# Order of the kept chunks' dK and dV, larger stores and a regrouped last chain in a fused attention-and-MLP backward pass

## The chip, the cores and the metric

The kernel runs on one core of one Trainium2 chip. The metric is the device time of one execution in microseconds (us); times quoted are medians. Every execution of the two kernels and of the experiments fell in the fast state, with two exceptions, both of run e10, that are named there and left out of the comparison.

## The reference

The forward pass is two layers of attention and MLP, used twice with the same weights; the kernel returns the output and all gradients.

```python
# B=2, one new token each, D=1024, F=3584, 32 query heads, 4 key/value heads, 16384 cached keys, head size 128
def attn(x, K, V, wq, wo):                 # K, V: (2, 4, 16384, 128) bf16
    q = heads(x @ wq)
    p = softmax(q @ repeat(K).T * 128 ** -0.5)
    return merge(p @ repeat(V)) @ wo
def mlp(x, w1, b1, w2, b2):
    return gelu(layernorm(x) @ w1 + b1) @ w2 + b2
def f(x, K, V, wq, wo, w1, b1, w2, b2):
    for _ in range(2):
        x = x + attn(layernorm(x), K, V, wq, wo)
        x = x + mlp(layernorm(x), w1, b1, w2, b2)   # normalized here and again inside
    return x
out, vjp = jax.vjp(f, ...)
return out, *vjp(grad_out)   # output 1 = dx, 2 = dK, 3 = dV, 4 = dWq, 5 = dWo, 6..9 = dw1, db1, dw2, db2
```

dK and dV have the size of the caches (33.5 MB each). They and the weight gradients are written in the last pass over the caches, while K and V are read once more.

## The kernel before

The last pass begins at about 740 us. It works in **steps**. A step has two slots, and a streamed chunk of V (1 MB in bf16) takes four slots. There are 32 chunks. Four of them (numbers 0 to 3, the **kept** ones) are still on the chip from the pass before; the other 28 are **streamed**. For each slot PE transposes eight blocks of V, an engine copies them to `kT`, and eight products make dP. Each step also makes halves of dK chunks in its first slot and of dV chunks in its second, none, one or two in a slot as `k_at` and `v_at` below ask for it:

```python
X = [px([128, 512], F32, "xm%d" % i) for i in range(4)]      # four PSUM banks; mx() hands them out in turn

def kv_pair(w, i, h):                     # half h of chunk i of dV or dK
    g, c = chunks[i]
    if h == 0:
        stgs[w, i] = new_home()           # a 1 MB staging buffer
    ...
    pss = [mx() for _ in range(4)]        # all four banks
    for b in range(2):
        for r in range(4):
            PE.matmul(pss[r][:, b * 256:(b + 1) * 256], lhsT=blk[32 * r:32 * r + 32, o + 2 * h + b, :], ...)
    for r in range(4):
        evac_cast(sv_[:, 2 * h:2 * h + 2, r], pss[r][:]..., 512)    # a copy of 128x512, on DVE or ACT
    store(dst, <this half>, stgs[w, i] if h == 1 else None)         # 512 KB
```

The weight gradients are cut into **fill units**: one product of 128x512 into one of the same four banks, and one copy. Loads are issued by SP into whichever 1 MB buffer comes free, out of some sixteen that serve for loads and for staging alike; stores are issued by POOL. The loop, with what chooses the order:

```python
    v_at = {2 * i - 3: i for i in range(2, NC)}                  # step -> chunk of dV
    k_at = {(i - 1 if i < NCH else 2 * i - NCH - (i == NC - 1)): i for i in range(NC)}     # NCH = 4, NC = 32
    make_blks(None, 0)
    while ...:                            # m counts the steps
        for k in range(2):
            ...                           # transposes of V, kT, dP of the slot
            at, w, m_ = ((k_at, "K", m - 1), (v_at, "V", m))[k]
            for h in range(2):
                if at.get(m_ - h) is not None:
                    kv_pair(w, at[m_ - h], h)
            if tail:
                tail.popleft()()
        ...
        step_fill(1 if m < NCH else 5)    # fill units of this step
        pump(...)                         # loads, while buffers are free
        m += 1
```

The end of the pass is a chain: the last dP, the last quads of dq, their evacuation and reduction, the products `dn_tail` with Wq, a layer-norm backward, and output 1. It was driven by `sch.later(...)`, one or two steps later for each link, and by the list `tail`.

Of the kernel before, what the change touches and what calls it, by code (L numbers as in the profile page):

```python
# [9 lines left out]
BF16 = mybir.dt.bfloat16  # L10
# [13 lines left out]
def kernel(  # L24
# [25 lines left out]
    V = nc.vector  # L50
    S = nc.scalar
    PE = nc.tensor

    B, _, D = A_x.shape
# [972 lines left out]
            V.tensor_copy(out=diag[:, t], in_=gcols.unsqueeze(1).to_broadcast([128, 4, n]))  # L1027

    def q_make(w, g, bank):
        Qm = wrk2.tile([128, 2, 128], BF16, name="Qm" + w)  # L1030
        for t in range(2):
            PE.matmul(bank[:, t * 128:(t + 1) * 128], lhsT=spr[w][:, t * 128:(t + 1) * 128], rhs=ident[:],
                      start=True, stop=True)
        evac_cast(Qm[:].rearrange("p a b -> p (a b)"), bank[:, 0:256], 256)
        qms[w, g] = Qm
# [101 lines left out]
    def store(out_ap, view, tile_):  # L1137
        nc.gpsimd.dma_start(out_ap, view)
        if tile_ is not None:
            by_store.append(tile_)  # L1140
# [21 lines left out]
    def dw_units(xrows, yrows, i, chunks, y0, ny, out_of):  # L1162

        ps_, tpos = (slice(0, 128), None) if i is None else (slice(32 * i, 32 * i + 4), (32 * i, 0))
        box = {}
        units = []
        for j0, rb in chunks:
            for j in range(rb):
                for c0 in range(0, ny, 512):
                    def u(j0=j0, rb=rb, j=j, c0=c0):  # L1170
                        if j == 0 and c0 == 0:
                            box["t"] = new_home()
                        sv_ = box["t"][:, 0:rb * ny].rearrange("p (j n) -> p j n", j=rb)
                        ps = mx()
                        PE.matmul(ps[:], lhsT=xrows[ps_, (j0 + j) * 128:(j0 + j + 1) * 128],  # L1175
                                  rhs=yrows[ps_, y0 + c0:y0 + c0 + 512], start=True, stop=True, tile_position=tpos)
                        evac_cast(sv_[:, j, c0:c0 + 512], ps[:], 512)
                        if c0 + 512 >= ny and (j % 2 == 1 or j == rb - 1):
                            js = j - j % 2
                            store(out_of(j0 + js, j + 1 - js), sv_[:, js:j + 1], box["t"] if j == rb - 1 else None)  # L1180
                    units.append(Unit(u, j == 0 and c0 == 0))
        return units

# [63 lines left out]
    def kv_pair(w, i, h):  # L1247

        g, c = chunks[i]
        if h == 0:  # L1250
            stgs[w, i] = new_home()
        sv_ = stgs[w, i][:].rearrange("p (b r t d) -> p b r t d", r=4, t=2, d=128)
        blk, Qm = blks[w, i], qms[w, g]
        o = 0 if w == "V" else NB
        pss = [mx() for _ in range(4)]
        for b in range(2):
            for r in range(4):
                PE.matmul(pss[r][:, b * 256:(b + 1) * 256], lhsT=blk[32 * r:32 * r + 32, o + 2 * h + b, :],  # L1258
                          rhs=Qm[32 * r:32 * r + 32, :, :].rearrange("p a b -> p (a b)"), start=True, stop=True,
                          tile_position=(32 * r, 0))  # L1260
        for r in range(4):
            evac_cast(sv_[:, 2 * h:2 * h + 2, r], pss[r][:].rearrange("p (b t d) -> p b t d", b=2, t=2), 512)
        dst = (dVv if w == "V" else dKv)[g, :, c * TC + h * TC // 2:c * TC + (h + 1) * TC // 2, :]
        store(dst, stgs[w, i][:, h * LDW // 2:(h + 1) * LDW // 2].rearrange("p (t d) -> p t d", d=128),
              stgs[w, i] if h == 1 else None)

    dwq_v = out_4.rearrange("(j p) n -> p j n", p=128)
    quarters = {}
# [7 lines left out]
    def in_rows(q, kv):  # L1276
        box, ps = q[4], pm_([128, 512], F32, "dn_tail")

        def part(a):
            for j in range(a, a + 4):  # L1280
                for o in range(8):
                    PE.matmul(wide_out(ps, 2 * j), lhsT=box[j - j % 4][:, j % 4, o * 128:(o + 1) * 128],  # L1282
                              rhs=wide_in(dq_all[:, kv * 8 + o, 0:2]), start=(o == 0), stop=(o == 7))

        def last():
            V.tensor_tensor(out=dn0[:], in0=dn0[:], in1=pairs(ps, DJ), op=ALU.add)
            g0 = attn_in_bwd(0, g1, dn0, lambda: step_fill(1), lambda: step_fill(2))
            tail.append(lambda: col_to_row_f32(g0, DJ, out_1.rearrange("b s d -> (b s) d"), "o1",
                                               ktp.tile([128, 8, 128], BF16, name="o1", tag="kT")))

        return [lambda: part(0), lambda: part(4), last]

    def quarter(kv):

# [45 lines left out]
    def dq_quad(i, q):  # L1340
        g, c = chunks[i]
        accs[g].coef = lambda u: dX[i][:, u - c * CP, 0].rearrange("p h t -> p (h t)")
        accs[g].quad(c, q)
        if q == 1:
            if g == G - 1:
                by_read.append(held_tiles["K%d" % c])
            else:
                done("K", g, c)

    def score0(s):  # L1350
        i, b = NCH + s // NB, s % NB
        g, c = chunks[i]
        if b == 0:
            dps["t"] = pm_([128, 16, TC], F32, "dp")
        scores(i, b, kTs.pop(s), dps["t"])
        if b < NB - 1:
            return
        if c == 0:
            open_dq(g)
        if order.index(g) % 2 == 1 and c == (2 if i < 2 * NCH else 0):  # L1360
            quarter_loads(g % HKV)
        ds0(i, dps["t"][:])
        end = 1 if i == NC - 1 else 2
        sch.later(1, lambda: dq_quad(i, 0))
        sch.later(end, lambda: dq_quad(i, 1))
        if c == NCH - 1:
            sch.later(end, accs[g].evac)
            sch.later(end + 1, accs[g].reduce)

    def step_fill(n):  # L1370
        for k in range(n):
            for q in ((late, fill) if k % 2 == 0 else (fill, late)):
                if q and q[0].ready():
                    q.popleft()()
                    break
# [53 lines left out]



    v_at = {2 * i - 3: i for i in range(2, NC)}
    k_at = {(i - 1 if i < NCH else 2 * i - NCH - (i == NC - 1)): i for i in range(NC)}
    make_blks(None, 0)
    NS = (NC - NCH) * NB
    zero = {}
    m = 0
    while 2 * m < NS + 12 or late or fill or late_pe or tail or m <= max(v_at) + 2:
        sch.s = m
        qs = []  # L1440
        iv, ik = v_at.get(m + 1), k_at.get(m)
        for w, i in (("V", iv), ("K", ik)):
            if i is not None and chunks[i][1] == 0 and (w, chunks[i][0]) not in qms:
                qs.append(make_qm(w, chunks[i][0]))
        for k in range(2):
            s = 2 * m + k
            if s < NS:
                i, b = NCH + s // NB, s % NB
                cv = get("V", *chunks[i])[:].rearrange("p (t d) -> p t d", d=128)
                kT = ktp.tile([128, 8, 128], BF16, name="kT", tag="kT")  # L1450
                tp = mtp()
                for j in range(8):
                    PE.transpose(tp[:, j, :], cv[:, b * 8 + j, :], ident[:])
                evac_bf16(kT[:].rearrange("p a b -> p (a b)"), tp[:].rearrange("p a b -> p (a b)"), 1024)
                kTs[s] = kT
                if b == NB - 1:
                    done("V", *chunks[i])
                if b == 0 and chunks[i][1] == 0:
                    wg = chunks[i][0]
                    V.tensor_copy(out=wide_do[wg][:, :, 3], in_=cols["V"][:, wg].rearrange("p l r -> p (l r)"))  # L1460
            if 0 <= s - 2 < NS:
                score0(s - 2)
            if late_pe and (k == 1 or s >= NS or len(late_pe) > 6):
                late_pe.popleft()()
            at, w, m_ = ((k_at, "K", m - 1), (v_at, "V", m))[k]
            for h in range(2):
                if at.get(m_ - h) is not None:
# [3 lines that stand above are left out]
        for f in qs:  # L1471
            f()
        if iv is not None or ik is not None:
            make_blks(iv, ik)
        sch.run_slot(1)
        if m == NS // 2 - 8:
            zero["t"] = new_home()
            nc.gpsimd.memset(zero["t"][:, 0:2 * D], 0.0)
            nc.gpsimd.tensor_copy(out=zero["t"][96:100, 0:D], in_=rowsB[96:100, :])
        step_fill(1 if m < NCH else 5)  # L1480
        pump(NLD + 3 if m < NCH else NLD, 3)
        m += 1

# [29 lines left out]
```

## Time and profile before

| | before |
|---|---|
| median of 3 runs | 1141.74 us (1140.79 to 1143.36) |
| span of the profiled run, mean granted clock of PE | 1144.5 us, 0.852 |
| moved in it | 449.33 MB |
| busiest engine | PE, 83% of the span |

Three more views of this profile matter later. The first is one stretch, steps 9 to 32 of the last pass. Its columns are those of the stretches in the prediction: window, length, busy us (and instructions) of PE, PEld, DVE, ACT, POOL, then granted clock, DMA share, GB/s.

```profile
801.60:955.20 153.60, 136.13 (x1835) 84.26 (x1834) 121.48 (x216) 113.75 (x218) 41.35 (x72) 0.84 1.02 418
```

A step takes 6.4 us here (153.6 / 24), and DVE is busy for 79% of it, ACT for 74%.

The second is the list of what engines waited for from 800 us on (total us, times, longest). The two largest lines in which a copying engine waits for a store to land are these (two more, for `keepK`, have 2.3 and 2.1 us):

```profile
ACT big L161 <- DMA out_dram<-big: 15.7, 3, 11.7
DVE big L164 <- DMA out_dram<-big: 13.6, 2, 11.1
```

So before, the copies were at times ahead of the DMA and stood waiting for a free staging buffer. But none of these waits lies in steps 9 to 32: all are between 955 and 1107 us, and 11.7 and 11.1 us of them are one stall of both engines at 1061 to 1072. The third view is the summary of the chain that ended last, as shares of the span. The whole chain is short: followed back from the end it reaches only to 1105.8 us, and at 1108.3 the landing of a store holds it for 2.88 us:

```profile
PE 1%; DVE 1%; issue 0%; DMA 0%; ACT 0%; POOLq 0%; DVEq 0%; ACTq 0%
```

### The profile page before, as it was taken

The page shows a single profiled execution, that of the slowest core. Times are in us where ns is not written, and L with a number is a line of the kernel's source. Part 1 is how long each engine was busy: PE and PEld are TensorE (multiplying, and loading weights), DVE is VectorE, ACT ScalarE, POOL GpSimd, SP SyncE. Part 2 cuts the span into 40 slices and gives each one's busy share as a digit, 9 for nine tenths or more (in the row PEclk, how much of TensorE's full clock was granted, in tenths as well). Part 3 has the DMA queues.
Part 4 walks back from the last instruction along what each step waited for, and adds up shares of the span by engine and source line. Part 5 has one row for each costly group of instructions (what it writes and reads, how often), then busy time and mean ns, then how long its engine had stood idle before and what let it go on. Part 6 is the DMA issues. An engine that isn't in the chain of part 4 may idle for free. (4 is left out here: it accounts for less than half of the span.)

```text
span 1144.5 us, 40256 instructions
## 1 busy us (share of the span) xinstructions
PE 949.9 (83%) x17565; PEld 733.8 (64%) x17567; DVE 633.3 (55%) x1357; ACT 564.7 (49%) x1415; POOL 117.9 (10%) x206
## 2 busy tenths in 40 slices
PE   4988796488879875899997789889898989998586
PEld 3867674487767765888776688765555555555352
DVE  1545442133545433454845355768778877887485
ACT  0544352022535430344454454657767867777473
POOL 0000000000000000000000000012232322222323
PEclk9988886597999975899997799978878888988795
DMA  9999999998999989999999899987999999999997
GB/s 374 423 424 425 424 424 412 406 377 359 425 424 423 424 320 423 390 373 408 368 417 421 340 359 355 352 347 276 411 421 420 420 417 415 388 407 403 417 401 292
DMA packets 98717, 449.33 MB, mean 393 GB/s; under 512 B 8418, under 2 KB 8418, under 8 KB 67564
## 3 DMA queue, kind: packets, MB, share of 16 engines
q1 hardware_dynamic: 72204, 348.17, 75.6%
q0 software_dynamic: 26336, 98.60, 21.2%
q8 instruction: 137, 2.24, 0.7%
q14 instruction: 40, 0.33, 0.1%
HBM read 348.14 MB, written 98.58 MB: 390 GB/s over the span
## 5 line engine op out<-in xcount | busy, mean ns | idle before, releaser
L153 ACT COPY kT<-tp 128x512 int32<-128x512 int32 x209 | 122.7, 588 | 252.5 <-PE tp L420 246.0
L156 DVE COPY kT<-tp 128x1024 bf16<-128x1024 bf16 x159 | 108.7, 690 | 109.6 <-PE tp L420 100.4
L420 PE MATMUL tp<-ident,kv_K 128*128 128x128 bf16 x1728 | 141.3, 229 | 5.0 <-DMA kv_K<-in_A_k_cache_dram 4.6
L420 PEld LDWEIGHTS <-kv_K 128*128 128x128 bf16 x1728 | 107.1, 102 | 6.0 <-DMA kv_K<-in_A_k_cache_dram 5.3
L164 DVE CAST big<-xm 128x512 bf16<-128x512 f32 (+1 forms) x125 | 80.8, 684 | 33.2 <-DMA out_dram<-big 13.6
L161 ACT CAST big<-xm 128x512 bf16<-128x512 f32 (+1 forms) x139 | 75.6, 594 | 37.1 <-DMA out_dram<-big 15.7
L573 PEld LDWEIGHTS <-kT 128*128 128x128 bf16 x2048 | 76.0, 98 | 27.4 <-issue 21.5
L573 PE MATMUL sc<-qT_bf,kT 128*128 128x8 bf16 x2048 | 91.7, 171 | 0.3 <-issue 0.3
L270 PE MATMUL wtp<-ident,wt 128*128 128x128 bf16 x928 | 76.2, 230 | 3.7 <-issue 2.4
L420 PE MATMUL tp<-ident,kv_V 128*128 128x128 bf16 x864 | 71.1, 230 | 8.3 <-DMA kv_V<-in_A_v_cache_dram 6.8
L537 ACT ACTIVATE e_all<-sc,negm 128x64 bf16<-128x64 f32 x256 | 77.1, 345 | 1.1 <-DVE negm L532 1.0
L161 ACT CAST keepV<-xm 128x512 bf16<-128x512 f32 x118 | 64.7, 594 | 24.8 <-PE xm L1258 18.5
L306 PEld LDWEIGHTS <-wt 128*128 128x128 bf16 x1696 | 48.8, 103 | 42.6 <-issue 15.2
L452 PE MATMUL acc_all<-kv_V,e_all 128*16 128x256 bf16 x864 | 46.4, 295 | 28.5 <-DMA kv_V<-in_A_v_cache_dram 15.2
L156 DVE COPY wT<-wtp 128x1024 bf16<-128x1024 bf16 (+1 forms) x64 | 40.7, 640 | 47.7 <-PE wtp L270 44.1
L164 DVE CAST keepK<-xm 128x512 bf16<-128x512 f32 (+1 forms) x87 | 56.4, 684 | 18.3 <-PE xm L1258 9.7
L153 ACT COPY wT<-wtp 128x512 int32<-128x512 int32 (+1 forms) x60 | 34.3, 572 | 63.6 <-PE wtp L270 55.2
L164 DVE CAST keepV<-xm 128x512 bf16<-128x512 f32 x86 | 55.7, 683 | 15.1 <-PE xm L1258 8.5
L420 PEld LDWEIGHTS <-kv_V 128*128 128x128 bf16 x864 | 56.3, 103 | 10.1 <-DMA kv_V<-in_A_v_cache_dram 8.1
L270 PEld LDWEIGHTS <-wt 128*128 128x128 bf16 x928 | 58.3, 103 | 4.3 <-issue 2.9
L161 ACT CAST keepK<-xm 128x512 bf16<-128x512 f32 (+1 forms) x95 | 51.7, 590 | 18.3 <-PE xm L1258 14.2
L537 ACT ACTIVATION_READ_ACCUMULATOR e_all<-sc,negm 128x1 f32 x256 | 60.1, 235 | 0.0
(368 smaller groups left out, 1845.8 us busy)
## 6 DMA issues: line engine op xcount, KB each, us to landing
kv_K<-in_A_k_cache_dram SPq DMA_DIRECT2D x81, 1024.0 KB, 11.7
kv_V<-in_A_v_cache_dram SPq DMA_DIRECT2D x81, 1024.0 KB, 12.2
wt<-in_A_wo_dram SPq DMA_DIRECT2D x32, 1024.0 KB, 10.1
out_dram<-big POOLq DMA_DIRECT2D x62, 512.0 KB, 15.0
wt<-in_B_w_dram SPq DMA_DIRECT2D x32, 896.0 KB, 14.2
out_dram<-keepV POOLq DMA_DIRECT2D x44, 512.0 KB, 13.8
out_dram<-keepK POOLq DMA_DIRECT2D x42, 512.0 KB, 15.2
wt<-in_A_wq_dram SPq DMA_DIRECT2D x16, 1024.0 KB, 9.0
```

The lines of the kernel that those rows point to most:

```text
L153: S.copy(out=dst.bitcast(I32), in_=src.bitcast(I32))
L156: V.tensor_copy(out=dst, in_=src)
L161: S.copy(out=dst, in_=src)
L164: V.tensor_copy(out=dst, in_=src)
L270: PE.transpose(tp[:, o, :], wv[:, j, (o0 + o) * 128:(o0 + o + 1) * 128], ident[:])
L306: PE.matmul(fps[:, jo, :].rearrange("p (a b) -> p a b", b=2), lhsT=wv[:, j, jo * 128:(jo + 1) * 128], rhs=xT_bf[:, j0 + j, :].unsqueeze(1) ...
L420: PE.transpose(tp[:, j, :], cv[:, b * 8 + j, :], ident[:])
L452: PE.matmul(self.acc[cg:cg + 16, :], lhsT=coef(u), rhs=self.cv[:, t:t + 2, :].rearrange("p t d -> p (t d)"), start=False, stop=True, tile_ ...
L537: S.activation(out=e_all[:, g, f * half:(f + 1) * half, l, h, :], in_=sc[g][f][:, h, :].rearrange("p (a b) -> p a b", b=2), func=ACT.Exp, ...
L573: PE.matmul(sc[g][f][:, :, t % TH], lhsT=kT[:, j, :], rhs=q_bf[:, g, :], start=True, stop=True)
```

## The change

There are three parts. **(1)** The dV and dK of streamed chunks come first, so that the first steps turn loaded buffers over quickly; the six kept pieces that remain (dK 0 to 3, dV 2 and 3) are spread over steps 10 to 29, and the weight gradients wait until step 9. **(2)** Many stores are of 1 MB, not 512 KB. **(3)** The last chain is put into the list `tail`, which is emptied at one more place in each half step, and four unused products of 256 columns follow each piece that is taken there, to keep PE's clock up.

```diff
 def q_make(w, g, bank):
-    Qm = wrk2.tile([128, 2, 128], BF16, name="Qm" + w)
+    Qm = (vec if g == g0_ else wrk2).tile([128, 2, 128], BF16, name=("Q0" if g == g0_ else "Qm") + w)
 # dw_units
-    if c0 + 512 >= ny and (j % 2 == 1 or j == rb - 1):
-        js = j - j % 2
-        store(out_of(j0 + js, j + 1 - js), sv_[:, js:j + 1], box["t"] if j == rb - 1 else None)
+    if j == rb - 1 and c0 + 512 >= ny:
+        store(out_of(j0, rb), sv_, box["t"])
 # kv_pair
-    store(dst, <one half>, stgs[w, i] if h == 1 else None)
+    n = TC if 2 <= i < NC - 2 else TC // 2
+    if h == 1 or n < TC:
+        ...
+        store(dst, <the whole chunk, or the half>, stgs[w, i] if h == 1 else None)
 # in_rows
-    return [lambda: part(0), lambda: part(4), last]
+    return [lambda: (part(0), part(4)), lambda: None, last]
 # score0
-    end = 1 if i == NC - 1 else 2
+    if i == NC - 1:
+        tail.append(lambda: (dq_quad(i, 0), dq_quad(i, 1), accs[g].evac()))
+        tail.append(accs[g].reduce)
+        return
     sch.later(1, lambda: dq_quad(i, 0))
-    sch.later(end, lambda: dq_quad(i, 1))
+    sch.later(2 if i < NC - 2 else 1, lambda: dq_quad(i, 1))
     ...
 # the loop
-v_at = {2 * i - 3: i for i in range(2, NC)}
-k_at = {(i - 1 if i < NCH else 2 * i - NCH - (i == NC - 1)): i for i in range(NC)}
-make_blks(None, 0)
+v_at = {2 * i - 7: i for i in range(NCH, NC)}
+k_at = {2 * i - NCH - 2: i for i in range(NCH, NC)}
+for i in range(NCH):
+    k_at[9 + 6 * i] = i
+for i in range(2, NCH):
+    v_at[4 + 8 * i] = i
     ...
+            if tail:
+                tail.popleft()()
+                for _ in range(4):
+                    PE.matmul(ACCT[:, 0:256], lhsT=ident[:], rhs=<256 columns of e_all>, ...)   # result unused
             at, w, m_ = ((k_at, "K", m - 1), (v_at, "V", m))[k]
     ...
-        step_fill(1 if m < NCH else 5)
+        if NCH <= m < 2 * NCH + 1:
+            fill.popleft()()
+        step_fill(0 if m < 2 * NCH + 1 else 5)
```

More of the change, by code (lines that the diff above doesn't have):

```diff
@@ L1262, in kv_pair @@
             evac_cast(sv_[:, 2 * h:2 * h + 2, r], pss[r][:].rearrange("p (b t d) -> p b t d", b=2, t=2), 512)
-        dst = (dVv if w == "V" else dKv)[g, :, c * TC + h * TC // 2:c * TC + (h + 1) * TC // 2, :]
-        store(dst, stgs[w, i][:, h * LDW // 2:(h + 1) * LDW // 2].rearrange("p (t d) -> p t d", d=128),
-              stgs[w, i] if h == 1 else None)
+        n = TC if 2 <= i < NC - 2 else TC // 2
+        if h == 1 or n < TC:
+            t0 = h * n if n < TC else 0
+            dst = (dVv if w == "V" else dKv)[g, :, c * TC + t0:c * TC + t0 + n, :]
+            store(dst, stgs[w, i][:].rearrange("p (t d) -> p t d", d=128)[:, t0:t0 + n], stgs[w, i] if h == 1 else None)
     dwq_v = out_4.rearrange("(j p) n -> p j n", p=128)
@@ L1362, in score0 @@
         ds0(i, dps["t"][:])
-        end = 1 if i == NC - 1 else 2
+        if i == NC - 1:
+            tail.append(lambda: (dq_quad(i, 0), dq_quad(i, 1), accs[g].evac()))
+            tail.append(accs[g].reduce)
+            return
         sch.later(1, lambda: dq_quad(i, 0))
-        sch.later(end, lambda: dq_quad(i, 1))
+        sch.later(2 if i < NC - 2 else 1, lambda: dq_quad(i, 1))
         if c == NCH - 1:
-            sch.later(end, accs[g].evac)
-            sch.later(end + 1, accs[g].reduce)
+            sch.later(2, accs[g].evac)
+            sch.later(3, accs[g].reduce)
     def step_fill(n):
@@ L1464 @@
                 late_pe.popleft()()
+            if tail:
+                tail.popleft()()
+                for _ in range(4):
+                    PE.matmul(ACCT[:, 0:256], lhsT=ident[:], rhs=e_all[:, 0, 0:8, :, :, :].rearrange("p a l h t -> p (a l h t)"),
+                              start=False, stop=True, skip_group_check=True)
             at, w, m_ = ((k_at, "K", m - 1), (v_at, "V", m))[k]
```

## The prediction

> **What bounds the kernel now.** I first read the table of busy time in 40 slices: from the first slice to the last the row of the DMA stands at 9 in nearly every slice, while no engine is full throughout. So the kernel is a stream of 449 MB, and what can be won is the time in which that stream is not full. Then I cut the last pass (the one the change touches, from about 740 us) into stretches. The columns are busy time of PE, PEld, DVE, ACT and POOL, then the granted clock, the DMA share and the GB/s:
>
> ```profile
> 740.00:750.00 10.00, 8.26 (x115) 6.55 (x104) 5.87 (x16) 4.58 (x11) 1.59 (x3) 0.71 1.00 403
> 750.00:800.00 50.00, 44.85 (x637) 29.76 (x634) 38.05 (x66) 36.01 (x71) 11.59 (x21) 0.85 0.80 296
> 800.00:1107.00 307.00, 265.81 (x3572) 163.84 (x3565) 234.63 (x415) 219.58 (x421) 84.44 (x140) 0.84 1.02 411
> 1107.00:1130.00 23.00, 18.43 (x196) 8.66 (x194) 14.96 (x28) 13.40 (x26) 9.08 (x17) 0.63 0.99 400
> 1130.00:1144.50 14.50, 5.62 (x25) 1.90 (x24) 6.58 (x19) 3.69 (x7) 3.31 (x5) 0.61 0.48 195
> ```
>
> The reader is to see two holes around a full middle. Over 307 us the DMA share is 1.02 and 411 GB/s move; PE is busy 87% of it, DVE 76%, ACT 72%, so they have slack. From 750 to 800 only 296 GB/s move: 50 x (1 - 296/411) = 14.0 us of DMA time lost. From 1130 to the end 195 GB/s: 14.5 x (1 - 195/411) = 7.6 us lost. Everything else in the pass loses under 1 us. A perfect last pass would thus save about 21.6 us at the present rate.
>
> The waits of the DMA queue's own sequencer (SP) from 740 to 830 say why the first hole is there:
>
> ```profile
> SPq L1207 <- DMA out_dram<-big: 27.0, 2, 18.8
> SPq L1207 <- DMA out_dram<-keepV: 19.6, 3, 11.1
> SPq L1207 <- DMA out_dram<-keepK: 19.0, 1, 19.0
> SPq L1207 <- DMA out_dram<-keepxV: 10.2, 1, 10.2
> ```
>
> Loads (L1207) wait, up to 19 us at a time, for a store to land, because the 1 MB buffer they go into is still a staging buffer. The timeline of SP shows ten loads issued by 740.3 and then only four until 801.4 (759.8, 779.1, 789.9, 801.4). The first steps of the pass compute dK and dV of the chunks held on chip, then dW too, all of which take buffers for staging and free none by reading a streamed chunk. The same steps are long: the pairs of transposed V slots start at 749.5, 757.2, 763.8, 770.9, 777.0, 782.9, that is 6.7 us a step, with up to three half chunks of dV or dK copied in a step.
>
> The end, from the chain that ended last (start, duration, what):
>
> ```profile
> 1107.20 0.23 PE dp L1321
> ...
> 1108.26 2.88 DMA out_dram<-keepK
> ...
> 1118.53 0.99 PE xm L467 x4
> ...
> 1125.22 0.96 PE dn_tail L1282 x32
> ...
> 1127.07 0.96 PE dn_tail L1282 x32
> ...
> 1135.17 1.01 PE o L199 x4
> ```
>
> From the last dP product to the last store it is 37.3 us: 1107.2 to 1144.5. The dq reduction (L467), the two halves of the dn products and the transposes of output 1 stand with other work between them, and the clock there is 0.61 to 0.63.
>
> **What the skill says.** (1) "DMA: Bandwidth & Descriptors", section "Where 436 GB/s comes from": the ports carry 435 GB/s, and HBM may bind at some 358. Here 411 is held for 307 us, so the lower figure does not bind in this case and 411 is already 94% of the port figure: larger stores can add little. (2) The same page, "Why small descriptors are slow": a fixed overhead of about 3 cycles a packet. The packet records of this trace agree in kind: between 800 and 1130 a stored packet of 4096 B took 160.5 ns in the mean and one of 7168 B 273.5, which is 0.0368 ns a byte and 9.8 ns fixed; loads of 2048 and 8192 B (84.4, 328.0 ns) give 3.2 ns fixed. (3) "TensorE: Matmul & The Clock Gate", section "Part 1: The HAM clock gate": idle PE falls to half clock and some 3.4 us of activity bring it back. The trace agrees with the direction (0.61 in the tail, 1.00 in 690 to 740); its wake-up time I have not measured.
>
> **The change, part by part.**
>
> *Streamed chunks first.* Before, a step (two slots) up to number 4 made a dV half and up to two dK halves, all of kept chunks, and fill units began at once: one a step, five from step 4. Now steps 0 to 8 carry one dV and one dK half of streamed chunks, no dW, and only the five units that transpose rows; kept dK come at steps 9, 15, 21, 27, kept dV at 20 and 28. Copies a step in those nine steps: 8 of 128x512 at 0.684 (DVE) or 0.594 (ACT), two of 128x1024 at 0.690 or as halves 2 x 0.588, one block of the same size and a dS product of about 0.7 every other step: (8 x 0.64 + 3 x 0.75 + 0.35)/2 = 3.9 us on each engine, so with PE's waits I reckon 4.7 to 5.3 us a step in place of 6.7. Traffic a step is then 1 MB loaded and 1 MB stored: 2.1 MB / 5 us = 420 GB/s, so the DMA is about full from the moment stores flow. What stays of the hole is its start: dV0 and dV1 are stored from the same places as now, the ten early loads are done by about 750, and the first 1 MB of a streamed chunk is stored only at the end of step 2, near 757. I book 5 us lost there and 2 for steps that compute holds: 7 of the 14.0 remain, gain 7. The instruction order confirms that the same ten loads come first and that the next two go into buffers of dV0 and dV1, where before the next went into that of dK0.
>
> *Stores of 1 MB in place of 512 KB.* POOL has 64 queue rows fewer. POOL is no bound (84.4 of 307 us busy in the middle). Packets: 98.6 MB less 7.3 MB in 7 KB rows is 22,280 packets of 4 KB; some 2,050 stay, the others become 10,100 pairs, each saving 9.8 ns if the fixed part is paid once: 10,100 x 9.8 / 16 engines = 6.2 us. As 411 is so near the port figure I count half, 3 us. Against it: a buffer is held longer, by the half MB more that must land (about 2 us), and buffer V0 stays taken until step 28, one of some 16.
>
> *The tail.* The last dq quads, evacuation and reduction move from the ends of steps m+1 and m+2 into the next half steps, both dn halves are one piece (64 products), and four unused 256-column matmuls follow each piece. By the new order, from the last dP to output 1 stand 16 quads, 8 pair matmuls, the reduction, 8 + 4 transposes, 4 units, 64 products, 8 pair matmuls and 3 units. With the durations of the old chain (dq 0.8, evacuation and reduction 1.5, dq copies 0.5, rows 1.7, units 1.0, products 1.9, pairs 2, LN chain 4, transposes and copies 1.6, and waits) that is some 16 us against 30 (1107.2 to 1137.2). Behind it come 13 copies (13 x 0.64 / 2 = 4.2 us) and a last store of 1 MB, which needs about 6 us where 512 KB took 5.3 (1139.2 to 1144.5). So 26 us from last dP to end in place of 37. That is not all gain: the last dP itself comes later, since the bytes are the same and fewer stores are left behind it (I reckon 8 MB, four of them in flight, in place of 12). The measure is lost DMA time: 26 us hold 10.7 MB at 411, 8 move, 6.5 us lost, where 37.3 us lost about 8.5. Gain 2, and 1 more for the clock. The 24 unused matmuls cost 24 x 0.11 to 0.21 = 2.6 to 5 us of PE time, mostly while it waits for copies.
>
> *Sum:* 7 + 3 + 3 = 13 us off 1141.7: about **1128.5**.
>
> **Rivals.** *Buffers become the wait.* Larger stores hold buffers longer, and 11 us of PE already stand at 1061 to 1072 behind two copies that waited 11.7 and 11.1 us for stores to land. Against it: the DMA was at 1.03 during that very stall, so it cost nothing; only if it fell below full would it. It would give back some 5 to 10 us, time 1133 to 1140. *Compute becomes the bound.* The work taken out of steps 0 to 8 is added behind; PE is 87% busy. If it cannot follow, the gain of the hole is paid back later: 1136 to 1142. Against it: DVE and ACT under 77%, and PE's busy time is stretched by a clock of 0.84. Before, fill ran out near step 53 (no dW product between 1077 and the last quarter); now it should reach to the end. *The full gain.* No hole at all, the full 6 us of packets and a tail as short as its last store: 14 + 6 + 4 = 24, time 1118. For it speaks that the loads are six chunks ahead at 750. *The last store.* 1 MB behind the last copy could cost 2 us more than I booked.
>
> **Range and chances.** Most mass lies between the buffers rival and near the full gain: 1116 to 1139. Faster by over 2% means under 1119, which needs nearly all three gains whole: 0.12. Slower by over 2% needs a new stall of 36 us in a full stream: 0.02.
>
> **What would show it.** The stretch 750 to 800 at 340 to 390 GB/s, steps of about 5 us there, and more than four loads between 741 and 801; stored packets of 8192 B at about 311 ns and the middle at 414 to 418 GB/s; 24 to 28 us from last dP to end, and a clock in it above 0.65. The prediction is wrong if 750 to 800 stays at 300, if the middle shows a DMA share under 1.0 with loads waiting on stores, or if the packets of 8 KB take twice those of 4 KB.

## The result, and the profile after

| | before | changed |
|---|---|---|
| median, 4 runs each on one chip | 1142.55 us | 1157.01 us (1156.90 to 1164.02) |
| span of the profiled run, clock | 1144.5 us, 0.852 | 1155.2 us, 0.834 |

The ratio is 1.0141, with a 95% interval of 1.0098 to 1.0183. A ratio here is the mean time of one kernel's fast runs over that of the other's fast runs of the same rounds, so it is not quite the ratio of the medians. On a second chip the changed kernel gave 1.0100 (1.0064 to 1.0137; run f1 below). It is about 1 to 1.4% slower: within 2%, but 18 us above the upper end of the predicted range.

The stretches of the changed kernel that answer to the five in the prediction, cut at its own end:

```profile
740.00:750.00 10.00, 7.90 (x150) 5.67 (x147) 6.77 (x20) 5.10 (x11) 1.07 (x2) 1.00 0.93 357
750.00:800.00 50.00, 44.85 (x747) 31.66 (x743) 39.52 (x71) 37.07 (x72) 5.33 (x10) 0.90 0.90 337
800.00:1107.00 307.00, 270.61 (x3297) 162.38 (x3293) 229.87 (x396) 215.30 (x409) 49.01 (x80) 0.76 1.00 400
1107.00:1130.00 23.00, 18.83 (x276) 12.08 (x273) 16.85 (x30) 15.57 (x30) 5.26 (x9) 0.87 1.02 420
1130.00:1155.20 25.20, 12.35 (x112) 5.67 (x112) 9.89 (x23) 7.20 (x13) 3.15 (x5) 0.64 0.45 182
```

The early hole has shrunk: 337 GB/s from 750 to 800, where 296 moved before. SP's waits from 740 to 830, the view that explained the hole, are now these:

```profile
SPq L1206 <- DMA out_dram<-big: 32.6, 3, 13.3
SPq L1206 <- DMA out_dram<-keepV: 24.0, 3, 10.3
SPq L1206 <- DMA out_dram<-keepK: 20.7, 3, 9.9
```

Loads still wait for stores, no less in total, but no longer for 19 us at a time; the longest wait is 13.3, and more loads go out in between.

But the full middle is no longer full. It moves 400 GB/s in place of 411, and the clock has dropped from 0.84 to 0.76. Steps 9 to 32 of the changed kernel, the ones that now hold the kept pieces, show where:

```profile
780.80:973.60 192.80, 166.38 (x1955) 98.58 (x1956) 138.57 (x239) 129.66 (x247) 26.20 (x46) 0.71 0.98 376
```

These 24 steps begin 21 us earlier than before and end 18 us later. DVE and ACT have 52 instructions more (486 in place of 434, 12%), 48 of which must be the copies of the twelve kept halves; PE has 7% more, and the steps are 26% longer. Each engine is less busy than before: DVE 72%, ACT 67%, PE 86% (before 79%, 74%, 89%). So more work was added than fits, although no engine became full. The steps also move 72.5 MB in place of 64.2: of the 39 us by which they are longer, 20 are the time of these bytes at 411 GB/s, and the other 19 are lost. The DMA share, 0.98, hides this: a load packet of 8192 B took 366 ns in the mean in these steps, against 313 before (the median is 309 in both), so that fewer bytes kept the DMA engines nearly as busy.

The waits of the copying engines for stores, from 800 us on, in the changed kernel:

```profile
ACT big L161 <- DMA out_dram<-big: 3.0, 1, 3.0
DVE big L164 <- DMA out_dram<-big: 2.3, 1, 2.3
```

They fall from 29.3 to 5.3 us, and both lines are now in steps 9 to 32. The copies are no longer ahead of the DMA. The summary of the chain that ended last agrees. It no longer runs into the landing of a store; it goes back 243 us, to 912.4, through engines alone:

```profile
PE 14%; DVE 3%; ACT 3%; issue 1%; POOLq 0%; DVEq 0%; ACTq 0%
```

Its end, step by step (start, duration, what), answers to the chain of the prediction:

```profile
1126.32 1.04 PE xm L467 x4
...
1131.71 1.71 PE dn_tail L1283 x64
...
1139.42 1.03 PE o L199 x4
```

The last dP product is at 1121.5, so from there to the end are 33.7 us (before 37.3).

**An account of the DMA.** As in the prediction I count *lost DMA time*: the length of a stretch less the bytes moved in it at 411 GB/s. Here it is cut at the kernel's own events, and added up from the packets of one profile each. Before and the experiments e3, e6 and e11 do not differ in their opening steps, and gave 14.1, 7.6, 8.1 and 9.9 us there, so the first column is good to some 6 us only. The changed kernel and its repeat f1 agree to 0.6 us in the first three columns and differ by 3.5 in the last.

| lost, us | 740 to step 9 | steps 9 to 32 | step 33 to last dP | last dP to end | sum |
|---|---|---|---|---|---|
| before | 14.1 | -2.6 | 2.7 | 8.2 | 22.4 |
| changed | 4.8 | 16.4 | -3.2 | 13.9 | 31.9 |
| difference | -9.3 | +19.0 | -5.9 | +5.7 | +9.5 |

The difference of 9.5 us is close to that of the two profiled spans, 10.7 us; the medians of the result are 14.5 apart, since the profiled execution of before was a longer one (1146.27 us). The change won 3 to 9 us where it aimed (4.8 are left of 7.6 to 14.1), and lost more where it put the work. Behind step 33 the two last columns cancel.

### The profile page after: what moved, and what is told of

Same layout as the page of the kernel before. It is cut to its first block, busy times and chain, and to the rows that moved or that the text cites. A ratio compares the mean times of both kernels' runs of the same rounds, so it can differ in the third digit from the quotient of the medians.

```text
span 1155.2 us, 40027 instructions
## 1 busy us (share of the span) xinstructions
PE 958.4 (83%) x17577; PEld 739.7 (64%) x17579; DVE 635.2 (55%) x1355; ACT 567.2 (49%) x1418; POOL 71.7 (6%) x127
## 5 line engine op out<-in xcount | busy, mean ns | idle before, releaser
L161 ACT CAST big<-xm 128x512 bf16<-128x512 f32 (+1 forms) x150 | 80.9, 592 | 25.0 <-PE xm L1257 16.6
L164 DVE CAST big<-xm 128x512 bf16<-128x512 f32 (+1 forms) x117 | 76.2, 685 | 21.4 <-PE xm L1257 11.0
L161 ACT CAST keepV<-xm 128x512 bf16<-128x512 f32 x114 | 61.1, 591 | 27.3 <-PE xm L1257 22.9
L164 DVE CAST keepV<-xm 128x512 bf16<-128x512 f32 x93 | 60.6, 686 | 23.4 <-PE xm L1257 17.6
L161 ACT CAST keepK<-xm 128x512 bf16<-128x512 f32 x106 | 57.0, 591 | 18.6 <-PE xm L1257 15.0
L420 PEld LDWEIGHTS <-kv_V 128*128 128x128 bf16 x864 | 55.3, 102 | 13.8 <-DMA kv_V<-in_A_v_cache_dram 11.8
L164 DVE CAST keepK<-xm 128x512 bf16<-128x512 f32 x84 | 54.5, 685 | 16.4 <-PE xm L1257 11.6
## 6 DMA issues: line engine op xcount, KB each, us to landing
wt<-in_B_w_dram SPq DMA_DIRECT2D x32, 896.0 KB, 14.1
```

What stands on the lines that cost most here:

```text
L161: S.copy(out=dst, in_=src)
L164: V.tensor_copy(out=dst, in_=src)
L420: PE.transpose(tp[:, j, :], cv[:, b * 8 + j, :], ident[:])
```

## The experiments

The theory after this reading: **the kept pieces, put into steps that were already full, make compute the bound there** (the theory of compute). Its rivals are that larger stores or the longer use of buffers hold things up (buffers), that the drop of PE's clock is the cause rather than a symptom (clock), and that the unused products or the regrouped chain cost the time (tail).

### The parts alone: e1, e2, e3, e4

Four kernels ran on one chip: the larger stores alone (e1), the order alone (e2), the tail with its unused products alone (e3), order and tail without the larger stores (e4). Each takes the named hunks of the diff above and leaves the others as before.

```diff
 # e1: before, with the hunks of dw_units and kv_pair only
 # e2: before, with the hunks of q_make, v_at, k_at, make_blks and step_fill only
 # e3: before, with the hunks of in_rows, score0 and "if tail" only
 # e4: e2 and e3 together
```

> The kernel before with only the 1 MB stores. Order theory (the work moved out of the first nine steps overloads steps 9 to 32, and the stores are innocent): 1136 to 1144 us, stored 8 KB packets of about 313 ns. Buffer theory (a staging buffer held until a whole 1 MB lands starves the loads): at least 8 us slower than before, 1150 or more, with DMA share below 1.0 in the middle.

> The kernel before with only the new order of chunks and fill units (512 KB stores, old tail). Order theory: 1150 to 1160 us, steps 9 to 32 at about 8 us each as in the changed kernel. Buffer theory: the order alone fills the early hole and is faster, about 1130 us.

> The kernel before with only the new tail and the unused matmuls. Order theory: 1135 to 1143 us, last dP to end shorter than 37.3 us by some us. Tail theory (the unused matmuls sit in the way of the chain): slower by 3 us or more.

> The changed kernel with 512 KB stores back. Order theory: within 3 us of the changed kernel, 1152 to 1158 us. Buffer theory: back to 1140 or below.

| run | median us | ratio to before (95%) |
|---|---|---|
| e1 larger stores | 1144.11 | 1.0013 (0.9976 to 1.0051) |
| e2 order | 1149.95 | 1.0053 (1.0010 to 1.0097) |
| e3 tail | 1149.51 | 1.0048 (1.0005 to 1.0091) |
| e4 order and tail | 1155.02 | 1.0094 (1.0051 to 1.0137) |

The order alone is slower, and e2's profile has the changed kernel's shape: 2.6 us lost before step 9, 14.9 us in steps 9 to 32 (its six executions range from 1142.3 to 1153.8 us, and the profile is of one at 1152.2). The larger stores alone neither gain nor lose beyond the noise. The tail alone lost half a per cent in this set, but its six runs fall into two groups, near 1141 and near 1150 us (the profile is of a fast one), which I could not explain.

PE's timeline in steps 10 and 11 of e2 shows one way in which a kept piece can cost more than its work (start, duration, engine, line, operation; in brackets the idle time before it and what ended it). `Q0K` and `QmK` are the coefficients of a kept and of a streamed dK half:

```profile
785.88 0.40 PE L1258 MATMUL xm<-Q0K,blk 32*128 32x256 bf16 x8
786.94 1.48 PE L1258 MATMUL xm<-QmK,blk 32*128 32x256 bf16 x8 [0.67 <-ACT keepxK L161]
...
797.28 0.61 PE L1258 MATMUL xm<-QmK,blk 32*128 32x256 bf16 x8
798.56 1.38 PE L1258 MATMUL xm<-Q0K,blk 32*128 32x256 bf16 x8 [0.66 <-ACT keepV L161]
```

The first group of eight products takes 0.40 or 0.61 us. The second group of the same slot wants the same four banks. It stands for 0.66 us until the first copy is done, and then is paced by the copies: 1.4 to 1.5 us. During that time PE does nothing else, and the copying engines in turn wait for the products. In e2 the ten steps with a kept half (10, 11, 16, 17, 20 to 23, 28, 29) took 6.6 to 12.6 us, 99.6 together, where the same step numbers before took 5.0 to 9.5, 66.6 together: 33 of the 38 us by which steps 9 to 32 of e2 are longer. In these ten steps no engine is busier than before (PE 86% in place of 89%, DVE 67% in place of 77%, ACT 63% in place of 72%), and the granted clock is 0.50 in five of them, where it was 0.71 or more before.

### Is it the clock? e5 and e6

The granted clock in the middle of e2 is lower than before. Here PE transposes every block of V twice in steps 9 to 32, so that it is busier and a higher clock may be granted; e5 does so on e2, e6 on the kernel before.

```diff
-                for j in range(8):
+                for j in [*range(8)] * (2 if 9 <= m < 33 else 1):
                     PE.transpose(tp[:, j, :], cv[:, b * 8 + j, :], ident[:])
```

> The order alone (as e2_order) with the eight transposes of each V slot done twice, into the same place, in steps 9 to 32: 384 matmuls of 128x128 more, same result. Clock theory (in these steps PE is the bound and its granted clock of about 0.7 is the cause): the clock in 800 to 950 rises to 0.85 or more and the time falls by 4 us or more against e2_order, to 1146 or below. Overload theory (the copies and the order of work bound these steps, the clock is a by-product): the added 20 to 35 us of PE work makes it slower, 1155 or more, or leaves it as it was at a higher clock.

> The kernel before with the same doubled transposes in steps 9 to 32. Clock theory: clock up from about 0.85 to 0.95, but the DMA is full in these steps, so the time stays within 3 us of before, 1139 to 1145. Overload theory: slower by 5 us or more.

Windows 800 to 950 and 950 to 1100 of e2, then 800 to 950 of e5 (columns as above):

```profile
800.00:950.00 150.00, 131.85 (x1537) 79.66 (x1536) 105.58 (x183) 99.26 (x189) 37.07 (x65) 0.69 0.99 384
950.00:1100.00 150.00, 134.91 (x1638) 81.26 (x1637) 116.24 (x202) 109.44 (x208) 46.59 (x76) 0.78 1.02 414
```

```profile
800.00:950.00 150.00, 129.61 (x1800) 87.20 (x1801) 104.53 (x181) 97.32 (x186) 36.34 (x63) 0.86 1.00 387
```

The clock rose from 0.69 to 0.86, as wanted, and the traffic stayed where it was: 387 against 384 GB/s. In time e5 is at 1155.56 us, ratio 1.0113 (1.0078 to 1.0149), no faster than e2 (on another chip); e6 is at 1.0020 (0.9993 to 1.0047). Within one kernel the executions with a lower mean clock are the longer ones (e2: 0.853 at 1142.3 us, 0.827 at 1153.7), but a higher clock made on purpose did not bring the traffic back: 15.3 us are lost in steps 9 to 32 of e5. Its ten steps with a kept half took 93.0 us in place of 99.6, and the other fourteen 99.8 in place of 92.1. The doubled transposes are themselves work for PE, so what a higher clock alone is worth stays open: a share of it in the steps with a kept half is not excluded, and that it is the main cause is not supported.

### Does the loss follow the kept pieces? e7

On e2, the kept dK move from steps 9, 15, 21, 27 to 33, 39, 45, 51, and the kept dV from 20 and 28 to 36 and 44.

```diff
-    for i in range(NCH):      k_at[9 + 6 * i] = i
-    for i in range(2, NCH):   v_at[4 + 8 * i] = i
+    for i in range(NCH):      k_at[33 + 6 * i] = i
+    for i in range(2, NCH):   v_at[20 + 8 * i] = i
```

> The order alone with the kept dK at steps 33, 39, 45, 51 and the kept dV at 36 and 44, in place of 9 to 27 and 20, 28. Overload theory (too much work packed into steps 9 to 32): these steps fall from 7.8 to about 6.9 us and the time by 4 us or more against e2_order, to 1146 or below. Clock theory: the clock stays near 0.7 and the time is that of e2_order, 1148 to 1154.

The two halves of the middle in e7:

```profile
800.00:950.00 150.00, 127.89 (x1723) 78.83 (x1723) 114.54 (x201) 107.62 (x205) 39.96 (x68) 0.83 1.02 415
950.00:1100.00 150.00, 135.33 (x1400) 79.12 (x1399) 103.51 (x175) 95.86 (x183) 42.24 (x69) 0.62 0.99 379
```

The slow stretch moved with the pieces: 415 GB/s from 800 to 950, where e2 has 384, and 379 from 950 to 1100, where e2 has 414. The lost time in steps 9 to 32 fell from 14.9 to 3.4 us, and from step 33 to the last dP it rose from -2.6 to 16.0. The longest steps are now 34 and 35 (16.7 and 11.8 us), and the twelve steps that now hold a kept half take 119.1 us, where the same step numbers in e2 take 75.0. The clock follows too, 0.83 and then 0.62. The order of the streamed chunks gives no reason for a loss that moves with these six pieces. Buffers could move with them, since a kept piece takes a staging buffer and frees none; e9 and e10 speak to that. In time e7 is at 1160.75 us, 1.0139 (1.0097 to 1.0181).

### Do the larger stores add to it? e8

The changed kernel without its tail hunks, that is order and larger stores.

```diff
 # e8: the changed kernel, with in_rows, score0 and "if tail" as before
```

> The changed kernel with the old tail and without the unused matmuls. If the parts add up (order +6, tail +5.5, stores +1.5 us as e1 to e3 measured) this is 1149 to 1152 us, 5 us below the changed kernel; if the stores hurt only together with the new order, 1153 or more.

1153.25 us, 1.0094 (1.0063 to 1.0124). Steps 9 to 32 lose 21.9 us in its profile, against 14.9 in e2; but the changed kernel and f1, with the same order and the same stores, lose 16.4 and 17.0. The interval overlaps that of e2, on another chip, so an extra cost of larger stores in this place is possible and not shown.

### Is it the copies? e9

On e2, the copies of kept pieces in the loop take 32 columns of 512. Products, banks, order and stores stay. The dK and dV of those chunks are wrong on purpose.

```diff
         for r in range(4):
+            if i < NCH and not opening["on"]:
+                evac_cast(sv_[:, 2 * h, r, 0, 0:32], pss[r][:, 0:32], 32)
+                continue
             evac_cast(sv_[:, 2 * h:2 * h + 2, r], pss[r][:]..., 512)
```

> The order alone with the copies of the kept dK and dV out of PSUM cut from 512 to 32 columns (dK and dV wrong on purpose; the same products, buffers and bytes stored). Copy theory (steps 9 to 32 are bound by products and copies that take turns at four PSUM banks): 48 copies of 0.64 us become about 0.1 us, some 13 us of each copy engine's time or more; the DMA time lost in these steps falls from 16 to under 8 us and the time to 1144 or below. Buffer theory (the loads starve because kept chunks hold staging buffers): unchanged, 1147 to 1154, and 14 us or more lost.

```profile
800.00:950.00 150.00, 129.52 (x1689) 79.51 (x1690) 109.02 (x207) 102.04 (x209) 41.06 (x71) 0.81 1.02 411
```

1143.83 us, 0.9993 (0.9978 to 1.0007, on another chip than e2, each against before on its own chip): the loss of e2 is gone. From 800 to 950, 411 GB/s move in place of 384, and the clock is 0.81 although nothing was done for it. Steps 9 to 32 take 175.5 us in place of 191.7, and lose 4.4 in place of 14.9. The ten steps with a kept half take 83.3 us in place of 99.6, the other fourteen 92.2 in place of 92.1. So shorter copies alone bring back the traffic, and the clock with it, though buffers and stored bytes are as in e2.

### Is it buffers? e10

One buffer is taken out of the pool of e2 before the loop.

```diff
     opening["on"] = False
+    by_read.popleft()
```

> The order alone with one 1 MB buffer taken out of use at the end of the opening. Buffer theory: clearly slower than e2_order, 4 us or more, with more DMA time lost in steps 9 to 32. Copy theory: within 3 us of e2_order, 1147 to 1153.

1151.49 us over six executions, 1.0075 (1.0045 to 1.0105). Two more, at 1168.43 and 2334.97 us, were in the slow state and are left out (the median of all eight is 1153.87). Its profile loses 13.8 us in steps 9 to 32, no more than e2 does (14.9). If buffers were what the steps lack, one less should have cost there. The total is 2 parts in a thousand above e2, with overlapping intervals on different chips: inconclusive for a small cost, and no support for buffers as the cause.

### The tail without the unused products: e11, and the fill hunk alone: e12

e11 is e3 without the four unused products. e12 is the kernel before with the `step_fill` hunk only, so that weight gradients wait until step 9 but kept pieces come first as before.

```diff
 # e11, on e3
             if tail:
                 tail.popleft()()
-                for _ in range(4):
-                    PE.matmul(ACCT[:, 0:256], ...)
 # e12, on before
-        step_fill(1 if m < NCH else 5)
+        if NCH <= m < 2 * NCH + 1:
+            fill.popleft()()
+        step_fill(0 if m < 2 * NCH + 1 else 5)
```

> e3_tail without the unused matmuls. If the unused matmuls cost the time: back to before, 1140 to 1143. If the pulled-forward chain does, by pushing the last dK and dV stores behind it so that the DMA runs dry: as e3_tail, 1146 to 1150, with 7 us or more of DMA time lost after the last dP.

> The kernel before with only the fill units moved: none in steps 0 to 3, one in steps 4 to 8, five after; kept dK and dV stay first. In before the fill runs out near step 49 and steps 50 to 56 have none, so 24 units find free room there. Copy theory: steps 0 to 8 get some 6 to 8 us shorter and nothing is given back, 1134 to 1139. Buffer theory: the kept chunks still hold the buffers in steps 0 to 8, the loads still starve, 1140 to 1145.

e11 is at 1145.48 us, 1.0014 (0.9999 to 1.0030), e12 at 1145.81, 1.0014 (0.9995 to 1.0033). In e12's profile the loss before step 9 is 4.2 us (7.6 to 14.1 with the old order of fill), so holding the weight gradients back already closes part of the early hole; but 4.2 us are lost in steps 9 to 32 (before: -2.6) and 12.3 after the last dP (before: 8.2). Here too what was put off came back later, though in steps 9 to 32 it costs less than the kept pieces do.

### The changed kernel once more, and two parts taken from it: f1, f2, f3, f4

These four ran on one chip: the changed kernel again (f1), without the unused products (f2), with e9's short copies (f3, wrong on purpose in the same outputs), and e2 with two fill units in place of five in the steps that hold a kept half, and one or two in the first nine steps to make up for it (f4).

```diff
 # f4, on e2
-        if NCH <= m < 2 * NCH + 1:
-            fill.popleft()()
-        step_fill(0 if m < 2 * NCH + 1 else 5)
+        kept = sum(0 <= at_.get(m - d - lag, NC) < NCH for at_, lag in ((v_at, 0), (k_at, 1)) for d in (0, 1))
+        step_fill(1 if m < 5 else 2 if m < 2 * NCH + 1 else 2 if kept else 5)
```

> The changed kernel itself, as the anchor of this chip: 1153 to 1160 us, 14 to 20 us of DMA time lost in steps 9 to 32 and 8 or more after the last dP.

> The changed kernel without the unused matmuls. If they hold up the last dK and dV behind them: 3 us or more below the changed kernel of the same rounds. If they are hidden in the waits of the chain: within 2 us.

> The changed kernel with the copies of the kept dK and dV cut to 32 columns (wrong on purpose). Copy theory: 6 us or more below the changed kernel, 1150 or less, and under 10 us lost in steps 9 to 32. If the 1 MB stores, by holding buffers, are a second cause beside the order: 12 us or more stay lost.

> The order alone with the fill units levelled: one a step in 0 to 4, two in 5 to 8, then five, but two in the steps that carry a kept half. Copy theory: the kept steps shorten by about 1 us for 3 units less, the lost DMA time of steps 9 to 32 falls from 16 to about 8 us, and the time to 1143 to 1149; it beats before only if the units fit into the last steps for nothing.

| run | median us | ratio to before (95%) | lost in steps 9 to 32 | lost after last dP |
|---|---|---|---|---|
| f1 changed | 1156.50 | 1.0100 (1.0064 to 1.0137) | 17.0 | 10.4 |
| f2 no unused products | 1157.05 | 1.0098 (1.0075 to 1.0120) | 14.7 | 8.3 |
| f3 short kept copies | 1146.78 | 1.0032 (1.0013 to 1.0051) | 5.6 | 13.2 |
| f4 order, levelled | 1152.71 | 1.0082 (1.0054 to 1.0111) | 3.3 | 18.1 |

f1 confirms the account on another chip. f2 equals f1: the unused products cost nothing that can be seen. f3 gives back 0.0068 of the ratio, 7.8 us of the 11.4 that the changed kernel loses here: most of its cost is in the kept pieces' copies. f4 took the loss out of the steps with kept pieces (3.3 us), and it came out in the first steps (8.1) and at the end (18.1). Its last stretches:

```profile
1120.00:1130.00 10.00, 8.11 (x90) 4.36 (x86) 4.54 (x9) 3.69 (x7) 1.27 (x2) 0.53 0.49 200
1130.00:1149.40 19.40, 6.93 (x23) 2.27 (x22) 7.36 (x20) 4.22 (x8) 4.13 (x6) 0.66 0.34 137
```

The DMA starves from 1120 on, with shares of 0.49 and 0.34. The work put off has to be done somewhere, and none of the placements tried found room for it. No kernel of the study that computes all outputs rightly was faster than the one before.

## Why the prediction was wrong, point by point

**The bound before was read rightly, the slack was not.** The pass was held by the DMA in its full middle: 418 GB/s at a share of 1.02 in steps 9 to 32. The prediction then read PE 87%, DVE 76% and ACT 72% as slack. It was enough to keep up, but not to take more: with 12% more copies and 13% more bytes the steps became 26% longer.

**The early hole: right.** Booked was a gain of 7 us with 7 left; 4.8 are left, and the gain is 9.3 against this profile of before, 3 to 9 against the four. The steps took 4.1 us (booked 4.7 to 5.3), seven loads went out from 741 to 801 in place of four (the first of them is the last of the ten early ones, which before went out at 740.3), and the window 750 to 800 moved 337 GB/s, just under the announced 340.

**The packets: right in size by luck, not seen in the time.** Between 800 and 1130 a stored packet of 8192 B took 314.8 ns (said: about 311), one of 4096 B 160.2, so a pair saves 5.6 ns, not 9.8; and there are 7,168 pairs, not 10,100. With the 1,264 small packets of 9.1 ns that also went, this is (7,168 x 5.6 + 1,264 x 9.1) / 16 = 3.2 us of DMA time. The 3 us that were booked were half of 6.2, for another reason. The profile of e1 loses 1.7 us less than that of before, and its timed runs show no gain (1.0013). One reading of the prediction is off: load packets of 8192 B took 323.7 ns in that window before, not 328.0, which makes the fixed part of a load 4.6 ns and not 3.2; nothing was built on it.

**The tail: wrong in sign.** Booked was a gain of 2, and 1 for the clock. From last dP to end I said 26 us; 33.7 and 33.0 (f1) were measured. The bytes left behind the last dP fell from 12.0 to 8.1 MB, as said, but because the stretch stayed that long, the lost time rose from 8.2 to 13.9 (10.4 in f1); booked was a fall from 8.5 to 6.5. One reason is a misreading of the diff: the new place at which `tail` is emptied is *added*, and I took it as moved. The pieces so come two to a half step, and the trace has 12 unused products, not 24. The tail's hunks lengthen the stretch wherever they are put in: 42.7 us (e3) and 40.2 (e11) against 37.3 before, 33.2 (e4) against 27.5 (e2). How much of the time of the kernel this makes is not settled: e11 puts it at 0.1%, e3 at 0.5%, in two groups of runs. The last 1 MB store took 6.7 us from issue (1148.5) to the end, as I had reckoned (6). The unused products are hidden, as said (f2).

**The step that failed: the sum booked 0 for the work put behind step 9.** The rival "Compute becomes the bound" was named, with its right cause ("the work taken out of steps 0 to 8 is added behind"), and put aside against two averages. Even it was sized at 1136 to 1142 only: it gave back the gain and no more. Measured, steps 9 to 32 with the twelve kept halves became 39 us longer, and 32 of these lie in the ten steps that hold one (98.5 us in place of 66.6). Of the 39 us, 20 are the 8.3 MB that moved in from other stretches; the rest is DMA time lost, 16.4 us in place of -2.6 (17.0 in f1): 19.0 us, or 1.6 a half, where 0 were booked. The averages could not show it: had the DMA stayed full, the 72.5 MB would have taken 176 us, and DVE would have been busy for 79% of them and ACT for 74%, just as before. One thing that the traces show in these steps is turn-taking: a slot with two halves, and fill units behind them, asks for four banks that the other half still holds. The Trainium skill ("PSUM — Partial Sum Buffer", section "PSUM bank collisions raise a hardware error") asks for PSUM to be guarded by bank, in the simple version of its rule. Here a bank has to be waited for in any case until its values are copied out, and the timeline of e2 shows two such waits: 0.66 and 0.67 us of idle PE, each before a second group of 1.4 to 1.5 us in place of 0.4 to 0.6.

**What is shown and what is not.** Shown: the loss comes with the order (e2), follows the kept pieces (e7), and is for the most part given back when only their copies are shortened (e9: 10.5 of the 17.5 us that e2 loses more than before in steps 9 to 32; f3). Not shown: how much of the copies' cost is bank waiting and how much is engine time, since short copies cut both; what part the low clock has in it, since it rises again when the copies are short; what makes the 7.0 us that e9 still loses more than before in these steps; why e3 has two groups of runs; and how the remaining 0.3% of f3 divides between the tail, the stores and the 5.6 us that it still loses in steps 9 to 32.

## What to carry to other kernels

Before work is moved from a stage where the DMA idles into one where it is full, count what a step of the full stage already holds of the resource that passes from hand to hand (here four PSUM banks between PE and two copying engines); average shares of 72 to 87% did not tell whether there was room, and the few steps that take the work have to be looked at by themselves. Copies that wait for stores are a sign of room only in the stage in which they wait: here the 29 us lay between 955 and 1107, and none in steps 9 to 32, where the work was put. And a lost-time account cut at the kernel's own events, rather than at fixed times, tells a gain that was given back later from one that never came.

## What the Trainium skill lacked or had wrong

- "DMA: Bandwidth & Descriptors", section "Where 436 GB/s comes from": its warning says that some 358 GB/s of HBM bind for transfers between HBM and SBUF; only a note further up ties that figure to both cores of the pair streaming, and the warning should repeat it. With one core running, 418 GB/s were held for 153.6 us of mixed loads and stores, so 358 did not bind here.
- "TensorE: Matmul & The Clock Gate", section "Part 4: PE-mode transpose": it says that transposes do not bring the full clock, as they do not count as busy PE in the same way. Doubling only the transposes of V (e5; bf16 in, bf16 out to PSUM) raised the granted clock from 0.69 to 0.86, and from 0.84 to 0.93 on the kernel before (e6, 800 to 950). The profile lists these as MATMUL; that they run in the mode that the page means is not shown.
- No page that I read prices the hand-over of PSUM banks between a group of products and its copies: in e2 PE stood idle for 0.66 and 0.67 us at the two turns shown, and the changed kernel lost 1.6 us of DMA time for each half chunk (19.0 us for twelve) in steps that were already full.
